# Weight conversion moved out of the last expert slot, softplus of two chunks ahead of a loop

## The chip, the cores and the metric

The kernel runs on 1 core of one Trainium2 chip. The metric is the time of one execution in microseconds (us) of device time. Six engines or queues matter here: TensorE (PE) for matrix products, VectorE (DVE), ScalarE (ACT) and GpSimd (POOL) for elementwise work, and SyncE (SP), which issues most DMAs.

## The reference

Three networks stand one behind the other. An attention over 32 memory slots per head (8 batches, 8 heads, 576 positions) gives 4608 rows of 512 numbers. A router picks one of 8 experts per row, and the expert is a two-layer network, `gate * (relu(x @ w1[e]) @ w2[e])`, with 1024 hidden units. Last comes a network that all rows share:

```
h = x @ w_in            # 4608 x 512 by 512 x 2048
g = max(h, 0) + log1p(exp(-|h|))
out = g @ w_out         # 2048 x 512
```

The weights `w_in` and `w_out` come in as 64-bit floats and have to be made 32-bit floats on the chip. "Conversion" below is this work.

## The kernel before, in words

Products are made exact enough by splitting each operand into a high and a low part and adding three products (`mm3`, L64): lines L67, L68 and L69 are its three matmuls. `split` (L55) makes the parts: ScalarE copies the high part (L58), VectorE or GpSimd subtracts it for the low part (L61).

**Experts** (`experts`, L649 on). Rows are sorted by expert. Eight units of 512 rows (s = 0 to 7) and two slots of 256 rows (s = 8 and 9, `LAST` is 9) are written out as one long list of 80 steps (s, n), n = 0 to 7 being chunks of 128 hidden units. Inside `tc.manual_schedule()` every engine works in the order in which the code is written. A step x holds:

- the first layer of its chunk on TensorE (12 matmuls into a PSUM tile `ph`), then the relu: ScalarE writes the high half of `h` (L125), VectorE the low half (L126);
- weight parts for the next unit: `part(0, m)` splits first-layer weights with VectorE's help, `part(1, m)` second-layer weights with GpSimd's, and loads for the unit after that;
- in steps n = 0 and 1, transposes and splits of the next unit's rows (`turn`, L675); in step n = 2, on SyncE, the loads of the rows of the unit after the next, with register loads ahead of them (`rows_of`);
- one `next(conv)`, in s = 1 to 7 and in s = 9;
- the second layer (`layer2`, tile `py`) of the step two earlier (`LAG = 2`); after a unit's last chunk, `slot_out` scales its rows on ScalarE (L693), GpSimd adds a column (L694) and SyncE stores them (L696).

**Conversion** (`convert`, L714). There are 32 halves of 128 x 512 numbers. Each takes two `yield`s, and the end of a half falls to the call after its second one. A call of the first kind finishes the half before (VectorE L729, which reads GpSimd's sum; then the store to `wsc` L712, or for the first six halves a split into the resident tiles `first`), asks for the load of the half after this one (L706, tile `d`, 2 buffers), and starts its half: VectorE L723 and L724, then ScalarE's Abs (L725), which overwrites what L724 reads. A call of the second kind is VectorE L726 and L727, then GpSimd's add (L728). With 32 halves this makes 64 yields and a 65th call that ends the last half. In the kernel before, units 1 to 7 make 56 calls, slot 9 makes 8, and the rest runs behind the steps.

**The loop** (L820) handles further slots of 256 rows, from a count that routing found on the chip (`nslots`). With these inputs the trace shows no turn of it; all engines meet there all the same, and SyncE also meets the DMAs issued ahead of it. Ahead of it stand the first layers of chunks 0 and 1 of the last network (`begun`, L818).

**The last network** (`last_network`, L872) works through 9 blocks of 512 rows with 16 chunks each: `layer3` (12 matmuls), softplus (three ScalarE operations L908 to L910, four VectorE operations L912 to L915, a split), and two chunks later `layer4` (12 matmuls). During block 0 it loads the weights of chunk 3 and on from `wsc` in halves (L895, tile `s`, 3 buffers under the tag `yt`) and splits them into tiles that the experts have left.

Of the kernel before, what the change touches and what calls it, by code (L numbers as in the profile page):

```python
# [1 line left out]

# [7 lines left out]
F32 = mybir.dt.float32  # L10
F32R = mybir.dt.float32r
BF16 = mybir.dt.bfloat16
I32 = mybir.dt.int32
AF = mybir.ActivationFunctionType
ALU = mybir.AluOpType
# [4 lines left out]
P = 128  # L20
# [4 lines left out]
DM = H * D  # L25
# [3 lines left out]
GC = FF // P  # L29
SLOT = 256  # L30
UNIT = 512
UNITS_E = 8
# [104 lines left out]
@with_exitstack  # L137
def tile_kernel(ctx, tc, qT, kv, phi, mid, wg, mbias, w1, w2, wffn, out):
    nc = tc.nc
    V, A, G, PE, SP = nc.vector, nc.scalar, nc.gpsimd, nc.tensor, nc.sync  # L140

    dram = ctx.enter_context(tc.tile_pool(name="dram", bufs=1, space=DRAM))
    cst = ctx.enter_context(tc.tile_pool(name="cst", bufs=1))

    xs = dram.tile([E * RG, ROW], F32, name="xs")
    ys = dram.tile([PAD + NT, ROW], F32, name="ys")
    wsc = dram.tile([GC, P, 2 * 4 * P], F32, name="wsc")

    A.preload_act_table_set("natural_log_exp_and_others")
    big = ctx.enter_context(tc.tile_pool(name="big", bufs=1))  # L150
    K = lambda i, shape, dt: big.tile([P, *shape], dt, name=f"k{i}", tag="k", bufs=12)
    Q = lambda i, shape, dt: big.tile([P, *shape], dt, name=f"q{i}", tag="q", bufs=3)
    J = lambda i, shape, dt: big.tile([P, *shape], dt, name=f"j{i}", tag="j", bufs=5)
    Z = lambda i, shape, dt: big.tile([P, *shape], dt, name=f"z{i}", tag="z", bufs=1)
    table = cst.tile([1, 4, TAB], I32, name="table")
    few = cst.tile([1, 7], I32, name="few")
    pick = [few[:, 0:3], few[:, 3:6]]
    nslots = few[:, 6:7]

    rows = ExitStack()  # L160
    ps_y = rows.enter_context(tc.tile_pool(name="ps_y", bufs=2, space=PSUM, side="right"))
    ig0 = cst.tile([P, 2, 2], F32, name="ig0")
    weights, py0 = attention_and_routing(tc, locals())
    act = ctx.enter_context(tc.tile_pool(name="act", bufs=1))
    raw = act.tile([P, UNIT // 32, P], F32, name="raw")
    hl = act.tile([P, 2, 2, 4, BLK], F32R, name="hl")
    fst = ctx.enter_context(tc.tile_pool(name="fst", bufs=1, side="right"))
    first = [[fst.tile([P, 1024], F32R, name=f"first{n}_{w}") for w in range(2)] for n in range(3)]
    ids = [act.tile([P, BLK // P], I32, name=f"ids{j}") for j in range(2)]
    idf = act.tile([P, BLK // P], F32, name="idf")  # L170
    ps_3 = ctx.enter_context(tc.tile_pool(name="ps_3", bufs=2, space=PSUM))
    begun = experts(tc, locals())
    rows.close()
    last_network(tc, locals())


# [472 lines left out]
def experts(tc, env):  # L649
# [5 lines left out]
    with ExitStack() as st:  # L655
        pool = lambda name, bufs, **kw: st.enter_context(tc.tile_pool(name=name, bufs=bufs, **kw))
        wk = pool("b_wk", 2)
        cv = pool("b_cv", 1)
        ps_h = pool("b_ps_h", 2, space=PSUM, side="right")

        W = env["weights"]
# [83 lines left out]
        with tc.manual_schedule():  # L745
# [26 lines left out]
            for x in range(len(steps) + LAG):  # L772
                if x < len(steps):
                    s, n = steps[x]
                    if x == 1:
                        slot_out([py0], ig0, PAD + NT - SLOT)
                    k = n - (3 if s == 0 else 0)
                    turned = [turn(s % 2, 2 * k + i, size(s + 1)) for i in range(2)] if s < LAST and k in (0, 1) else []
                    for t in turned:
                        next(t)  # L780
                    hs[x] = layer1((s + 1) % 2, n, size(s))
                    if s == 0:
                        for w, m in ((1, n), (0, n + 2)):
                            if m < FC:
                                part(w, m)
                                if m % 2 == 1 and (w, m) != (0, 1):
                                    load(w, m // 2, *regs[1])
                    for t in turned:
                        next(t)
                    if s + 2 <= LAST and k == 2:  # L790
                        rows_of(s + 2)
                        if s > 0:
                            expert_of(s + 2)
                    for w, ago in ((0, 2), (1, 4)):
                        if x >= ago and steps[x - ago][0] < LAST:
                            after, m = steps[x - ago]
                            part(w, m)
                            if m % 2 == 1 and after + 2 <= LAST:
                                load(w, m // 2, *regs[after + 2])
                    if s == LAST - 1 and n == 3:  # L800
                        block_in(tc, env, 0)
                    if s == LAST and 2 <= n < 6:
                        block_turn(tc, env, wk, 0, n - 2, 2)
                    if s == LAST and n == 6:
                        block_ids(tc, env, 0)
                    if 0 < s < UNITS_E or s == LAST:
                        next(conv, None)
                if x >= LAG:
                    s, n = steps[x - LAG]
                    if n == 0:  # L810
                        py[s] = [ps_y.tile([P, 2, DM], F32, name="py", tag="y") for _ in range(size(s) // SLOT)]
                    layer2(n, py[s], hs.pop(x - LAG))
                    if n == FC - 1:
                        slot_out(py.pop(s), igs.pop(s), PAD + NT - SLOT - UNIT if s == 0 else value(2, entry(s), PAD + NT - size(s)))
            for _ in conv:
                pass
            total = nc.values_load(nslots, min_val=TABU + SLOTS_E, max_val=TAB)
            begun = [layer3(tc, env, ps_3, first[n], 0) for n in range(2)]  # L818

        with tc.For_i(TABU + SLOTS_E, total, 1) as s:  # L820
            e = value(0, s, E - 1)
# [15 lines left out]
                if n + 2 < FC:  # L837
                    h.append(alone(n + 2))
            slot_out([pt], ig, y0)
    return begun  # L840


def layer3(tc, env, pool, w, j):
# [17 lines left out]
    tc.nc.vector.tensor_copy(env["ids"][j % 2], env["idf"])  # L861


def block_turn(tc, env, pool, j, k, bufs):
    nc = tc.nc
    raw, hl = env["raw"], env["hl"]
    yt = pool.tile([P, BLK], F32, name="yt", tag="yt", bufs=bufs)
    nc.vector.transpose(yt.rearrange("p (a b) -> p a b", b=32), raw[:, :, 32 * k:32 * k + 32])
    split(nc, yt, hl[:, (j + 1) % 2, 0, k], hl[:, (j + 1) % 2, 1, k], nc.scalar, nc.vector)


def last_network(tc, env):  # L872
    nc = tc.nc
    V, A, G, PE, SP = nc.vector, nc.scalar, nc.gpsimd, nc.tensor, nc.sync
    wsc, out, first, ids, ps_3, begun = (env[n] for n in ("wsc", "out", "first", "ids", "ps_3", "begun"))

    with ExitStack() as st:
        pool = lambda name, bufs, **kw: st.enter_context(tc.tile_pool(name=name, bufs=bufs, **kw))
        wp = pool("c_w", 1)
        wk = pool("c_wk", 2)  # L880
        ps_h = pool("c_ps_h", 2, space=PSUM)
        ps_o = pool("c_ps_o", 4, space=PSUM)
# [2 lines left out]
        q = [Q(6 + i, (2, 1024), F32R) for i in range(3)]  # L885
        room = [*(K(24 + i, (1024,), F32R) for i in range(12)), *(J(10 + i, (1024,), F32R) for i in range(5)),
                *(x[:, i] for x in q for i in range(2)), Z(2, (1024,), F32R)]
        room += [wp.tile([P, 1024], F32R, name=f"w{i}") for i in range(2 * (GC - len(first)) - len(room))]
        wh, wl = ([first[n][w] if n < len(first) else room[2 * (n - len(first)) + w] for n in range(GC)]
                  for w in range(2))  # L890

        def weights(n):
            for i in range(2):
                s, x = wk.tile([P, 512], F32, name="s", tag="yt", bufs=3), slice(512 * i, 512 * i + 512)
                SP.dma_start(s, wsc[n, :, x])  # L895
                split(nc, s, wh[n][:, x], wl[n][:, x], A, V)

        def hidden(j, n):
            if j == 0 and n < len(begun):
                ph = begun[n]  # L900
            else:
                ph = layer3(tc, env, ps_h if n % 4 // 2 else ps_3, (wh[n], wl[n]), j)
            u = wk.tile([P, BLK], F32, name="u", tag="u")
# [1 line left out]
            c = wk.tile([P, BLK], F32, name="c", tag="c", bufs=1)  # L905
            gh = wk.tile([P, BLK], F32R, name="gh", tag="gh", bufs=3)
            gl = wk.tile([P, BLK], F32R, name="gl", tag="gl", bufs=3)
            A.activation(u, ph, AF.Abs)  # L908
            A.activation(u, u, AF.Exp, scale=-1.0)  # L909
            A.activation(g, u, AF.Ln, bias=1.0)  # L910

            V.tensor_scalar(c, u, 1.0, 1.0, op0=ALU.add, op1=ALU.subtract)  # L912
            V.tensor_tensor(c, c, u, ALU.subtract)  # L913
            V.scalar_tensor_tensor(g, ph, 0.0, g, op0=ALU.max, op1=ALU.add)  # L914
            V.tensor_tensor(g, g, c, ALU.subtract)  # L915
            split(nc, g, gh, gl, A, V)
            return gh, gl

        def layer4(po, g, n):
# [3 lines left out]

        def block_out(j, po):
            for t in range(BLK // P):
                ob = wk.tile([P, DM], F32, name="ob", tag=("yt", "yt", "g", "g")[t], bufs=3)
                A.activation(ob, po[t], AF.Copy)  # L927
                w = G.indirect_dma_start(out, IndirectOffsetOnAxis(ap=ids[j % 2][:, t:t + 1], axis=0), ob, None,  # L928
                                         bounds_check=NT - 1, oob_is_err=False)
# [8 lines left out]
        for x in range(len(steps) + LAG):  # L938
            if x < len(steps):
# [4 lines left out]
                if j + 1 < NBLK:  # L944
# [1 line left out]
                        block_in(tc, env, j + 1)  # L946
                        block_ids(tc, env, j + 1)
                    if n in (6, 8, 10, 12):
                        block_turn(tc, env, wk, j + 1, (n - 6) // 2, 3)
            if x >= LAG:  # L950
                j, n = steps[x - LAG]
                if n == 0:
# [40 lines left out]
```

## Time and profile before

| what | value |
|---|---|
| time, three runs | 1411.44, 1412.92 (median), 1417.55 us |
| profiled execution | 1422.22 us, of which 1420.2 us span |
| mean granted TensorE clock | 0.976 of full |
| PE busy | 1370.2 us (96% of the span) |
| DVE busy | 922.5 us (65%) |
| ACT busy | 674.6 us (48%) |
| POOL busy | 256.9 us (18%) |
| chain that ended last | PE 50%, issue 6%, all else below 1% each |

The stages in the profiled execution, read from the timeline: attention and routing until about 190 us, the units s = 0 to 7 until about 548 us, the slots s = 8 and 9 until 603.76 us, the loop and its neighbours until 618.88 us, the last network to the end. An engine's busy time is an average over these stages; the windows view shows each stage by itself, and the timeline gives for each instruction how long its engine idled before it and what ended that. In rows a step of the units is followed best by its relu on VectorE (L126), of which there is one per step.

### The profile page before, as it was taken

The page shows a single profiled execution, that of the slowest core. Times are in us where ns is not written, and L with a number is a line of the kernel's source. Part 1 is how long each engine was busy: PE and PEld are TensorE (multiplying, and loading weights), DVE is VectorE, ACT ScalarE, POOL GpSimd, SP SyncE. Part 2 cuts the span into 40 slices and gives each one's busy share as a digit, 9 for nine tenths or more (in the row PEclk, how much of TensorE's full clock was granted, in tenths as well). Part 3 has the DMA queues.
Part 4 walks back from the last instruction along what each step waited for, and adds up shares of the span by engine and source line. Part 5 has one row for each costly group of instructions (what it writes and reads, how often), then busy time and mean ns, then how long its engine had stood idle before and what let it go on. Part 6 is the DMA issues. An engine that isn't in the chain of part 4 may idle for free.

```text
span 1420.2 us, 19794 instructions
## 1 busy us (share of the span) xinstructions
PE 1370.2 (96%) x7312; PEld 1100.9 (78%) x7312; DVE 922.5 (65%) x1699; ACT 674.6 (48%) x1193; POOL 256.9 (18%) x267
## 2 busy tenths in 40 slices
PE   7997989999999999889999999999999999999997
PEld 5775758878888888668888888888888888888885
DVE  4665857777877775769665756657566575665553
ACT  3554435444443445356544545445454454544443
POOL 1343314333434334300100101001010010100101
PEclk8889989999999999999999999999999999999998
DMA  9975984445334566244010200202001020000000
GB/s 357 402 285 202 374 240 102 104 113 140 95 99 127 170 213 182 89 143 133 23 38 0 60 1 23 38 0 60 1 23 38 0 60 1 23 8 1 30 1 30
DMA packets 94338, 143.03 MB, mean 101 GB/s; under 512 B 16160, under 2 KB 54048, under 8 KB 94240
## 3 DMA queue, kind: packets, MB, share of 16 engines
q1 hardware_dynamic: 86320, 120.94, 28.5%
q0 software_dynamic: 5760, 19.17, 3.5%
q10 hardware_dynamic: 2160, 1.63, 0.4%
q8 instruction: 58, 0.95, 0.3%
q14 instruction: 40, 0.33, 0.1%
HBM read 122.28 MB, written 44.62 MB: 118 GB/s over the span
## 4 chain that ended last, share of the span: by engine, by line
PE 50%; issue 6%; POOL 0%; DMA 0%; ACT 0%; DVE 0%; POOLq 0%; SPq 0%
PE po L67 8%; PE po L69 8%; PE po L68 8%; PE ph L67 8%; PE ph L69 8%; PE ph L68 8%; POOL out L928 0%; DMA s<-wsc 0%; POOLq L989 0%; ACT u L908 0%; DVE g L914 0%; DVE c L913 0%; ACT u L909 0%; ACT g L910 0%; ACT k L58 0%
## 5 line engine op out<-in xcount | busy, mean ns | idle before, releaser
L67 PE MATMUL ph<-hl,k 128*128 128x512 f32 (+1 forms) x536 | 204.3, 381 | 8.2 <-ACT hl L58 5.4
L68 PE MATMUL ph<-hl,k 128*128 128x512 f32 (+1 forms) x536 | 204.3, 381 | 0.0
L58 ACT ACTIVATE gh<-g 128x512 fp32r<-128x512 f32 x144 | 91.0, 632 | 228.3 <-DVE g L915 228.0
L912 DVE TENSOR_SCALAR c<-u 128x512 f32<-128x512 f32 x144 | 61.5, 427 | 194.7 <-ACT u L909 185.2
L928 POOL DMA_INDIRECT out<-ob,ids x36 | 41.3, 1147 | 767.9 <-ACT ob L927 661.7
L69 PE MATMUL ph<-hl,k 128*128 128x512 f32 (+1 forms) x456 | 173.1, 380 | 0.0
L61 DVE TENSOR_TENSOR gl<-g,gh 128x512 fp32r<-128x512 f32 x144 | 99.2, 689 | 84.7 <-ACT gh L58 83.7
L908 ACT ACTIVATE u<-ph 128x512 f32<-128x512 f32 x144 | 86.1, 598 | 133.0 <-PE ph L69 128.1
L67 PE MATMUL py<-q,h 128*128 128x512 f32 x304 | 121.7, 400 | 6.9 <-ACT h L125 5.9
L67 PEld LDWEIGHTS ph<-hl,k 128*128 128x128 f32 x536 | 101.6, 190 | 31.4 <-ACT hl L58 8.2
L69 PE MATMUL py<-q,h 128*128 128x512 f32 x304 | 120.7, 397 | 0.8 <-DVE h L126 0.8
L68 PEld LDWEIGHTS ph<-hl,k 128*128 128x128 f32 x536 | 101.6, 190 | 21.3 <-DVE hl L61 1.8
L126 DVE SCALAR_TENSOR_TENSOR h<-ph,h 128x512 fp32r<-128x512 f32 (+1 forms) x88 | 54.2, 616 | 82.6 <-ACT h L125 82.4
L913 DVE TENSOR_TENSOR c<-c,u 128x512 f32<-128x512 f32 x144 | 99.6, 692 | 4.5
L915 DVE TENSOR_TENSOR g<-g,c 128x512 f32<-128x512 f32 x144 | 99.0, 688 | 4.2
L914 DVE SCALAR_TENSOR_TENSOR g<-ph,g 128x512 f32<-128x512 f32 x144 | 98.3, 684 | 0.9 <-ACT g L910 0.9
L69 PEld LDWEIGHTS ph<-hl,k 128*128 128x128 f32 x456 | 85.7, 188 | 16.3
L125 ACT ACTIVATE h<-ph 128x512 fp32r<-128x512 f32 (+1 forms) x88 | 47.3, 537 | 107.4 <-PE ph L69 101.1
L909 ACT ACTIVATE u<-u 128x512 f32<-128x512 f32 x144 | 90.8, 631 | 4.0
L910 ACT ACTIVATE g<-u 128x512 f32<-128x512 f32 x144 | 90.8, 631 | 3.9
L67 PE MATMUL po<-k,gh 128*128 128x512 f32 x216 | 85.9, 398 | 0.0
L69 PE MATMUL po<-k,gl 128*128 128x512 f32 x216 | 85.5, 396 | 0.0
(236 smaller groups left out, 3083.7 us busy)
## 6 DMA issues: line engine op xcount, KB each, us to landing
k<-w SPq DMA_DIRECT2D x43, 512.0 KB
j<-w SPq DMA_DIRECT2D x43, 512.0 KB
k<-kv SPq DMA_DIRECT2D x36, 512.0 KB
d<-wffn SPq DMA_DIRECT2D x32, 512.0 KB
q<-qT SPq DMA_DIRECT2D x8, 1152.0 KB
raw<-ys SPq DMA_DIRECT2D x36, 256.0 KB
xs<-zero SPq DMA_DIRECT2D x8, 1056.0 KB
ys<-y SPq DMA_DIRECT2D x8, 1026.0 KB
```

The source lines that it names most:

```text
L58: hi_eng.activation(hi, x, AF.Copy)
L61: lo_eng.tensor_tensor(lo, x, hi.bitcast(F32), ALU.subtract)
L67: nc.tensor.matmul(out, lh, rh, start=start, stop=False)
L68: nc.tensor.matmul(out, lh, rl, start=False, stop=False)
L69: nc.tensor.matmul(out, ll, rh, start=False, stop=stop)
L908: A.activation(u, ph, AF.Abs)
L909: A.activation(u, u, AF.Exp, scale=-1.0)
L910: A.activation(g, u, AF.Ln, bias=1.0)
L912: V.tensor_scalar(c, u, 1.0, 1.0, op0=ALU.add, op1=ALU.subtract)
L913: V.tensor_tensor(c, c, u, ALU.subtract)
L914: V.scalar_tensor_tensor(g, ph, 0.0, g, op0=ALU.max, op1=ALU.add)
L915: V.tensor_tensor(g, g, c, ALU.subtract)
```

## The change

- Each of the units 1 to 7 makes a second `next(conv)` in step n = 3, units 1 and 2 make another one in step n = 6, and slot 9 makes none. That is 56 + 7 + 2 = 65 calls, so conversion ends with unit 7.
- The register loads of the loop's bound (`values_load`) move to step n = 6 of slot 9.
- The softplus of chunks 0 and 1 stands ahead of the loop, in written order, with tiles of the conversion's pool `cv` (tags a, b, c with one buffer each; results in tag d). The first layer of chunk 2 (`ready`) stands there too, as do three loads of weight halves for chunks 3 and 4 (`halves`), into the same tags a, b, c.
- The pool `cv` lives on into the last network. Its tags a, b, c in turn replace the three `yt` buffers, and two of its d buffers hold the last chunk's weights in place of the pool `wp`.

```diff
-    begun = experts(tc, locals())
+    cv = ctx.enter_context(tc.tile_pool(name="cv", bufs=1))
+    begun, ready, halves = experts(tc, locals())
...
                     if s == LAST and n == 6:
                         block_ids(tc, env, 0)
-                    if 0 < s < UNITS_E or s == LAST:
+                        total = nc.values_load(nslots, min_val=TABU + SLOTS_E, max_val=TAB)
+                    if 0 < s < UNITS_E:
                         next(conv, None)
+                        if n == 3 or (s < 3 and n == 6):
+                            next(conv, None)
...
-            for _ in conv:
-                pass
-            total = nc.values_load(nslots, min_val=TABU + SLOTS_E, max_val=TAB)
-            begun = [layer3(tc, env, ps_3, first[n], 0) for n in range(2)]
+            begun = []
+            for n in range(2):
+                ph = layer3(tc, env, ps_3, first[n], 0)
+                g = cv.tile([P, 2, BLK], F32R, name="g01", tag="d", bufs=2)
+                u, c, t = (cv.tile([P, BLK], F32, name=f"{x}01", tag=x) for x in "abc")
+                softplus(nc, ph, u, t, c, g[:, 0], g[:, 1])
+                begun.append((g[:, 0], g[:, 1]))
+            ready = [layer3(tc, env, ps_3, first[2], 0)]
+            halves = [scratch(env, 3 + i // 2, i % 2, i) for i in range(3)]
...
+def scratch(env, n, i, k):
+    s = env["cv"].tile([P, BLK], F32, name="s", tag="abc"[k % 3])
+    env["nc"].sync.dma_start(s, env["wsc"][n, :, 512 * i:512 * i + 512])
+    return s
+
+def softplus(nc, ph, u, g, c, gh, gl):
+    V, A = nc.vector, nc.scalar
+    A.activation(u, ph, AF.Abs)
+    A.activation(u, u, AF.Exp, scale=-1.0)
+    A.activation(g, u, AF.Ln, bias=1.0)
+    V.tensor_scalar(c, u, 1.0, 1.0, op0=ALU.add, op1=ALU.subtract)
+    V.tensor_tensor(c, c, u, ALU.subtract)
+    V.scalar_tensor_tensor(g, ph, 0.0, g, op0=ALU.max, op1=ALU.add)
+    V.tensor_tensor(g, g, c, ALU.subtract)
+    split(nc, g, gh, gl, A, V)
...
         def weights(n):
             for i in range(2):
-                s, x = wk.tile([P, 512], F32, name="s", tag="yt", bufs=3), slice(512 * i, 512 * i + 512)
-                SP.dma_start(s, wsc[n, :, x])
+                s, x = halves.pop(0) if halves else scratch(env, n, i, next(turns)), slice(512 * i, 512 * i + 512)
                 split(nc, s, wh[n][:, x], wl[n][:, x], A, V)
 
         def hidden(j, n):
             if j == 0 and n < len(begun):
-                ph = begun[n]
+                return begun[n]
+            if j == 0 and ready:
+                ph = ready.pop()
```

## Rows read from the trace of the kernel before

**Rows 1.** Windows: us, busy us of each engine (instructions), PE clock, DMA share, GB/s.
```profile
404.00:449.00 45.00, 45.00 (x197) 36.69 (x197) 35.27 (x46) 19.60 (x36) 18.32 (x14) 1.00 0.44 118
582.00:604.00 22.00, 15.29 (x68) 11.53 (x67) 15.16 (x28) 5.73 (x12) 5.22 (x5) 0.84 0.25 89
190.00:200.00 10.00, 9.87 (x25) 6.34 (x26) 4.68 (x7) 4.83 (x9) 1.91 (x2) 0.61 1.12 286
```

**Rows 2.** Timeline, TensorE, end of units and loop: start, us, operation, [idle before <-releaser].
```profile
593.22 0.50 PE L67 MATMUL py<-q,h 128*128 128x512 f32 x1 [2.13 <-ACT h L125]
...
601.04 0.79 PE L67 MATMUL py<-q,h 128*128 128x512 f32 x1 [2.76 <-ACT h L125]
...
603.76 0.48 PE L67 MATMUL ph<-hl,first 128*128 128x512 f32 x1
...
610.51 0.60 PE L68 MATMUL ph<-hl,first 128*128 128x512 f32 x1 [2.07 <-ACT u L908]
...
618.88 0.51 PE L67 MATMUL ph<-hl,k 128*128 128x512 f32 x1 [2.58 <-ACT k L58]
```

**Rows 3.** Timeline, ScalarE: two short steps, a conversion, the loop's exit.
```profile
566.70 0.39 ACT L125 ACTIVATE h<-ph 128x256 fp32r<-128x256 f32 x1 [1.40 <-PE ph L69]
...
569.52 0.39 ACT L125 ACTIVATE h<-ph 128x256 fp32r<-128x256 f32 x1 [1.40 <-PE ph L69]
...
592.24 0.65 ACT L725 ACTIVATE d<-d 128x512 f32<-128x512 f32 x1 [2.54 <-DVE b L724]
...
609.29 0.60 ACT L908 ACTIVATE u<-ph 128x512 f32<-128x512 f32 x1 [3.97 <-SPq L820]
```

**Rows 4.** Timeline, VectorE, units: second half of each relu, one row a step.
```profile
268.89 0.69 DVE L126 SCALAR_TENSOR_TENSOR h<-ph,h 128x512 fp32r<-128x512 f32 x1 [0.93 <-ACT h L125]
...
275.56 0.69 DVE L126 SCALAR_TENSOR_TENSOR h<-ph,h 128x512 fp32r<-128x512 f32 x1 [1.22 <-ACT h L125]
...
398.63 0.69 DVE L126 SCALAR_TENSOR_TENSOR h<-ph,h 128x512 fp32r<-128x512 f32 x1 [1.22 <-ACT h L125]
...
402.61 0.69 DVE L126 SCALAR_TENSOR_TENSOR h<-ph,h 128x512 fp32r<-128x512 f32 x1 [0.54 <-ACT h L125]
...
408.17 0.69 DVE L126 SCALAR_TENSOR_TENSOR h<-ph,h 128x512 fp32r<-128x512 f32 x1 [1.21 <-ACT h L125]
...
413.65 0.69 DVE L126 SCALAR_TENSOR_TENSOR h<-ph,h 128x512 fp32r<-128x512 f32 x1 [0.83 <-ACT h L125]
...
420.26 0.69 DVE L126 SCALAR_TENSOR_TENSOR h<-ph,h 128x512 fp32r<-128x512 f32 x1
...
425.14 0.69 DVE L126 SCALAR_TENSOR_TENSOR h<-ph,h 128x512 fp32r<-128x512 f32 x1 [0.23 <-ACT h L125]
...
430.89 0.69 DVE L126 SCALAR_TENSOR_TENSOR h<-ph,h 128x512 fp32r<-128x512 f32 x1 [1.22 <-ACT h L125]
```

**Rows 5.** Timeline, VectorE and GpSimd: conversion operations and what they waited for.
```profile
404.00 1.78 DVE L729 SCALAR_TENSOR_TENSOR c<-d,a 128x512 f32<-128x512 f32 x1
...
426.83 0.68 DVE L729 SCALAR_TENSOR_TENSOR c<-d,a 128x512 f32<-128x512 f32 x1
...
434.48 1.30 POOL L728 TENSOR_TENSOR a<-a,b 128x512 int32<-128x512 int32 x1 [1.15 <-DVE b L727]
...
439.52 0.43 DVE L723 TENSOR_SCALAR a<-d 128x512 int32<-128x512 int32 x1 [0.56 <-DMA d<-wffn]
```

**Rows 6.** Timeline, SyncE's queue: a chunk's load, the last store ahead of the loop.
```profile
433.69 0.42 SPq L706 DMA_DIRECT2D d<-wffn  x1
...
605.93 0.46 SPq L712 DMA_DIRECT2D wsc<-c  x1
```

**Rows 7.** Timeline, TensorE: the product that reads the relu of 430.89.
```profile
440.83 0.39 PE L69 MATMUL py<-q,h 128*128 128x512 f32 x1
```

**Rows 8.** Timeline, ScalarE and VectorE: one softplus near the kernel's end.
```profile
1401.35 0.60 ACT L908 ACTIVATE u<-ph 128x512 f32<-128x512 f32 x1 [1.18 <-PE ph L69]
...
1405.82 0.69 DVE L61 TENSOR_TENSOR gl<-g,gh 128x512 fp32r<-128x512 f32 x1 [0.70 <-ACT gh L58]
```

More of the change, by code (lines that the diff above doesn't have):

```diff
@@ L1 @@
+import itertools
 from contextlib import ExitStack
@@ L657, in experts @@
         wk = pool("b_wk", 2)
-        cv = pool("b_cv", 1)
+        cv = env["cv"]
         ps_h = pool("b_ps_h", 2, space=PSUM, side="right")
@@ L802, in experts @@
                     if s == LAST and 2 <= n < 6:
-                        block_turn(tc, env, wk, 0, n - 2, 2)
+                        block_turn(tc, env, wk, 0, n - 2, "yt", 2)
                     if s == LAST and n == 6:
                         block_ids(tc, env, 0)
-                    if 0 < s < UNITS_E or s == LAST:
+                        total = nc.values_load(nslots, min_val=TABU + SLOTS_E, max_val=TAB)
+                    if 0 < s < UNITS_E:
                         next(conv, None)
+                        if n == 3 or (s < 3 and n == 6):
+                            next(conv, None)
                 if x >= LAG:
@@ L839, in experts @@
             slot_out([pt], ig, y0)
-    return begun
+    return begun, ready, halves
+def scratch(env, n, i, k):
[12 more added lines that the diff above has]
+    split(nc, g, gh, gl, A, V)
 def layer3(tc, env, pool, w, j):
@@ L861, in block_ids, with block_turn @@
     tc.nc.vector.tensor_copy(env["ids"][j % 2], env["idf"])
-def block_turn(tc, env, pool, j, k, bufs):
+def block_turn(tc, env, pool, j, k, tag, bufs):
     nc = tc.nc
     raw, hl = env["raw"], env["hl"]
-    yt = pool.tile([P, BLK], F32, name="yt", tag="yt", bufs=bufs)
+    yt = pool.tile([P, BLK], F32, name="yt", tag=tag, bufs=bufs)
     nc.vector.transpose(yt.rearrange("p (a b) -> p a b", b=32), raw[:, :, 32 * k:32 * k + 32])
@@ L874, in last_network @@
     V, A, G, PE, SP = nc.vector, nc.scalar, nc.gpsimd, nc.tensor, nc.sync
-    wsc, out, first, ids, ps_3, begun = (env[n] for n in ("wsc", "out", "first", "ids", "ps_3", "begun"))
+    out, first, ids, ps_3, cv = (env[n] for n in ("out", "first", "ids", "ps_3", "cv"))
+    begun, ready, halves = (env[n] for n in ("begun", "ready", "halves"))
     with ExitStack() as st:
         pool = lambda name, bufs, **kw: st.enter_context(tc.tile_pool(name=name, bufs=bufs, **kw))
-        wp = pool("c_w", 1)
         wk = pool("c_wk", 2)
@@ L887, in last_network @@
                 *(x[:, i] for x in q for i in range(2)), Z(2, (1024,), F32R)]
-        room += [wp.tile([P, 1024], F32R, name=f"w{i}") for i in range(2 * (GC - len(first)) - len(room))]
+        room += [cv.tile([P, 1024], F32R, name=f"w{i}", tag="d", bufs=2) for i in range(2)]
         wh, wl = ([first[n][w] if n < len(first) else room[2 * (n - len(first)) + w] for n in range(GC)]
                   for w in range(2))
+        turns = itertools.count(len(halves))
         def weights(n):
             for i in range(2):
-                s, x = wk.tile([P, 512], F32, name="s", tag="yt", bufs=3), slice(512 * i, 512 * i + 512)
-                SP.dma_start(s, wsc[n, :, x])
+                s, x = halves.pop(0) if halves else scratch(env, n, i, next(turns)), slice(512 * i, 512 * i + 512)
                 split(nc, s, wh[n][:, x], wl[n][:, x], A, V)
@@ L907, in hidden @@
             gl = wk.tile([P, BLK], F32R, name="gl", tag="gl", bufs=3)
[L908 to L916, printed above, removed]
+            softplus(nc, ph, u, g, c, gh, gl)
             return gh, gl
@@ L925, in block_out @@
             for t in range(BLK // P):
-                ob = wk.tile([P, DM], F32, name="ob", tag=("yt", "yt", "g", "g")[t], bufs=3)
+                if t < 2:
+                    ob = cv.tile([P, DM], F32, name="ob", tag="abc"[next(turns) % 3])
+                else:
+                    ob = wk.tile([P, DM], F32, name="ob", tag="g", bufs=3)
                 A.activation(ob, po[t], AF.Copy)
@@ L948, in last_network @@
                     if n in (6, 8, 10, 12):
-                        block_turn(tc, env, wk, j + 1, (n - 6) // 2, 3)
+                        block_turn(tc, env, cv, j + 1, (n - 6) // 2, "abc"[next(turns) % 3], 1)
             if x >= LAG:
```

## The prediction

> **What bounds the kernel now.** I read the windows first, then the timelines of TensorE, ScalarE and VectorE where a window shows TensorE idle. Over one unit TensorE is busy all 45.00 us at full clock (197 matmuls, 0.23 us each), VectorE 35.27 and ScalarE 19.60 [rows 1]. So in the units TensorE sets the end and VectorE has a fifth of its time free. In 582 to 604 us, slot 9, TensorE is busy 15.29 of 22.00 us and its clock falls to 0.84 [rows 1]. The idle times there end with the relu on ScalarE: 2.13 and 2.76 us [rows 2]. ScalarE itself stood at the conversion's Abs, which waited 2.54 us for VectorE's L724 [rows 3]. So conversion bounds slot 9. Then comes the loop. The first matmul ahead of it is at 603.76, the flow stops until 610.51, stops again until 618.88 [rows 2], and ScalarE leaves the loop at 609.29 after 3.97 us for SyncE [rows 3]. From there on TensorE bounds. The change can win only between 570 and 619 us; it puts the work into the units.
>
> **Slot 9: what is removed.** Eight conversion calls leave it. A short step takes 2.82 us when nothing disturbs it (relus at 566.70 and 569.52, both waiting for TensorE), and the second relu is that of slot 9's step 0 [rows 3]. Seven more steps bring step 7's relu to 569.52 + 19.74 = 589.26; the second layers of steps 5, 6 and 7 are left, 18 matmuls at 0.23, so the first matmul ahead of the loop can come at 593.4. It came at 603.76 [rows 2]: **10.4 us** to win. It is all won if nothing else is late: block 0's transposes stay, about 2.4 us of VectorE in a step of 2.82 (relu, transpose, ScalarE's copy, remainder at 0.4 to 0.7 each). Lower bound: TensorE's idle time alone, 22.00 - 15.29 = 6.7 us [rows 1].
>
> **The units: what is added.** Seven units get one call more, the first two get two. The calls run on VectorE in written order, so the next step's relu stands behind them, and ScalarE's next relu stands behind the Abs, which waits for VectorE. What a step costs VectorE once it is behind is read from relu to relu [rows 4]:
> - a call of the second kind: 398.63 to 402.61 less 0.54 of waiting for TensorE's products: 3.44 us;
> - of the first kind: 402.61 to 408.17, 5.56 (with 1.21 at the end in which VectorE waits for Abs and relu); with a split into `first` 268.89 to 275.56, 6.67, so 1.1 more;
> - a unit's step 0 with a call of the first kind: 413.65 to 420.26, 6.61; step 1: 4.88; step 2: 5.75; step 7 with the next unit's transposes and a second-kind call: 408.17 to 413.65 less 0.83, 4.65.
>
> TensorE's step is half of 402.61 to 413.65, both waits for TensorE: 5.52 us [rows 4].
>
> In units 1, 2, 3, 5 and 7 the two calls of step 3 are a second kind and then a first kind (ten calls each in units 1 and 2, nine in 3 and on, counted from the first). They follow on each other directly, so VectorE waits for GpSimd's add: relu 430.89, add at 434.48, 1.30 long [rows 4, 5], so L729 can start 4.92 after the relu; with 0.71 L723 could start at 5.63, and from L723 to the next relu it is 441.9 - 439.52 = 2.38 (0.43, L724's 0.7, 1.21 of waiting). That makes 8.0 us. But L723 needs the load that step 2 asked for, behind the row loads on SyncE's queue: issued 433.69, and VectorE got on at 439.52 after waiting for it [rows 5, 6]. That is 8.63 after the relu of 430.89, not 5.63. SyncE's order is tied to VectorE's by GpSimd's add of step 1, behind which the rows' column and store stand, so the load moves with the delay. So step 3 takes 8.63 + 2.38 = **11.0 us**, 5.5 more than TensorE's. In step 6 of units 1 and 2 the load has had a step more: 8.0, in unit 1 with the split 9.1.
>
> How late may a relu be? That of 430.89 ended at 431.58, and the matmul that reads it ran at 440.83 [rows 4, 7]: 9.25, and it was 0.7 late itself: **9.9 us**. Adding up (step less 5.52): unit 1 from 0: step 3 +5.5, step 4 -2.1, 5 +1.2, 6 +3.6, 7 -0.9: 7.2 late. Unit 2: step 0 +2.2 (with a split), 1 -0.6, 2 +0.8, 3 +5.5, 4 -2.1, 5 0, 6 +2.5, 7 -0.9: 14.6. Unit 3: +1.1, -0.6, +0.2, +5.5: **20.8**, the peak, since from step 4 on units come out even or gain. TensorE loses 20.8 - 9.9 = **10.9 us**, in stops behind step 3 of units 2 and 3. Each stop brings a spell at half clock: 0.84 over 22 us is 7.0 us at half, two spells [rows 1], so up to 1.7 us each; only the last counts, and I take 1.2. Bounds: without the load wait the same walk (8.0 in step 3) peaks at 11.9, 2.0 us lost; with all slack held, 0; a gain is excluded, as TensorE is full there. I take 10.9, since the load's row is there in the trace.
>
> The row of L729 in that double step is a choice too: the same operation took 1.78 at 404.00 and 0.68 at 426.83 [rows 5]. I took 0.7, as in the double step it starts when GpSimd has just ended the add it waits for. The Trainium skill ("SBUF — State Buffer", section "SBUF: two separate sides") says that a VectorE operation with two SBUF operands and a GpSimd operation hold a shared port pair one at a time, the later one blocked for the whole instruction. By that rule 0.7 holds in a double step; priced at 1.78, step 6 of units 1 and 2 would add 2.2 and the sum would be 2.2 higher.
>
> **The loop: what is moved.** Count from T, the first matmul ahead of the loop. Now 36 first-layer matmuls are done and TensorE flows again at T + 15.1 (603.76 to 618.88) [rows 2]. Afterwards the same 36 stand ahead of the loop and take 8.3 us; the loop must not end before the two softplus and the three loads. Chunk 0's products are ready at T + 3.05 (12 at 0.23, 0.3 for the end). One softplus runs from 1401.35 to 1405.82 + 0.69: 5.16, and its copy to `gh` starts 0.70 ahead of the last part, at 3.8 [rows 8]. The second softplus on ScalarE starts behind that copy, at T + 3.05 + 4.3, and ends at T + 12.5. Its last tile, c, is the third load's target, so that load is issued at T + 12.6. At the loop all engines wait for SyncE, and SyncE for its DMAs: the last store went out at 605.93 and ScalarE was out at 609.29, 3.36 later, TensorE at 610.51, 4.58 later [rows 2, 3, 6]. TensorE comes early to the loop now, so I take 3.36: flow at T + 16.0, **0.9 later** than now. Bounds: -2.1 if the load's landing cost nothing, +2.1 with 4.58. What goes is the chain behind the loop (softplus, splits): the second layer of chunk 0 can start at once, and its 2.8 us cover the split of chunk 3. But TensorE has stood for 7 to 8 us. In 190 to 200, after the wait at the start of the units, the clock was 0.61 [rows 1], 7.8 us at half, which costs 3.9; a short stop costs 1.7. I take **2.8**. The first softplus also holds the PSUM buffer of chunk 2's products, for about 0.6 us, inside the wait.
>
> At nothing: three tags with one buffer each in place of three buffers of one tag, for the same rotation; two d buffers in place of the pool `wp`; the register loads a step earlier. TensorE's flow from 622 us on hides them; if a rotation stalled, a load of about 3 us per weight half would show in block 0. The two softplus taken out of block 0 free VectorE and ScalarE there, where TensorE bounds: nothing.
>
> **Sum.** -10.4 (slot 9) + 10.9 + 1.2 (units) + 0.9 + 2.8 (loop) = +5.4 us against the profiled execution, 1422.22 us (span 1420.2 and 2.0 around it), so 1427.6. The median of the runs is 1412.92, 9.3 below that execution; the difference carries over: **1418.3 us**, 0.4% slower, inside what a measurement can tell from no change (0.5%, 7 us).
>
> **Rivals.**
> 1. The units hide the calls. For it: VectorE has 9.7 us free per unit [rows 1], and without the load wait the walk loses 2.0. Against: the row of the wait [rows 5]. -10.4 + 2.0 + 0.9 + 2.8 = -4.7: 1408.2; with nothing lost and the loop at its lower price (-2.1, 1.7), down to 1402.1.
> 2. Slower: GpSimd. Its add in a double step stands behind its weight split (1.3 us), and L729 is held as at 404.00 (1.1 more). In step 3 the load's wait covers this, in step 6 of units 1 and 2 it doesn't: 2 x 2.4 = +4.9, and 1423.2. It decides as soon as a double step without load wait takes over 10 us, relu to relu. For it: 1.78 is a frequent length. Against: GpSimd's split starts ahead of the calls, so it should be done.
> 3. The loop gives nothing of the change's purpose back in another way: the loads hold it (4.58) and the clock stays low (3.9): +2.3 on the forecast, 1420.6; part of the slow side.
>
> **How the numbers follow.** The forecast (units lose 6 to 14 us) has 0.5, and by itself 1412 to 1422. Rival 1 has 0.3, rivals 2 and 3 together 0.2. Faster by over 0.5% means below 1405.9: half of rival 1, 0.15. Slower means above 1420.0: rivals 2 and 3 and the forecast's upper quarter, 0.33. The rest, 0.52, is no change. The range reaches from inside rival 1 to beyond rival 2: 1404 to 1426.
>
> **What would show it.** Slot 9 at full flow, 2.8 us a step; doubled steps of about 11 us between relus in step 3 of units 1, 2, 3, with a wait for the load of d at L723; TensorE idle for some 5 us in units 2 and 3, then low clock; TensorE's flow about 16 us behind T, starting with a second layer and at half clock. It is wrong if TensorE's windows in units 2 and 3 stay full, if L723 does not wait, or if the loop ends before T + 14.

## The result, and the profile after

The changed kernel takes 1430.76 us (median of 4 runs, 1429.91 to 1431.71), the kernel before 1412.18 (4 runs, 1411.37 to 1417.55): ratio 1.0128, 95% interval 1.0110 to 1.0147. It is 18.6 us slower; 5.4 were predicted. The profiled execution took 1429.91 us, span 1428.2. Its line numbers are one or two higher: the relus are L126 and L127, the row scalings L695, the conversion L725 to L731, the split L59 and L62.

Windows of the changed kernel (us, busy us of each engine, granted clock, DMA share, GB/s), the first two in the place of [rows 1]:

```profile
404.00:449.00 45.00, 45.00 (x197) 36.71 (x196) 37.03 (x46) 20.13 (x37) 18.35 (x14) 1.00 0.39 108
582.00:604.00 22.00, 22.00 (x142) 19.89 (x141) 10.10 (x18) 12.10 (x25) 10.29 (x10) 1.00 0.38 84
359.00:404.00 45.00, 40.48 (x168) 32.55 (x167) 36.22 (x45) 18.64 (x35) 17.85 (x13) 0.92 0.41 110
268.00:314.00 46.00, 37.62 (x156) 30.27 (x155) 34.13 (x46) 19.88 (x36) 16.78 (x13) 0.89 0.38 97
```

The slots are full now, at full clock. Some units are full as before. The other two windows lost 4.5 and 8.4 us of TensorE's time, with the clock at 0.92 and 0.89: 0.11 of 46 us is 10 us at the lower of the two levels. The waits between 222 and 560 us (engine, operation, what it waited for: us in total, times, longest) show what TensorE's stops have in common, first in the changed kernel, then in the kernel before:

```profile
ACT d L727 <- DVE b L726: 107.2, 26, 8.8
...
PE py L68 <- ACT y L695: 23.9, 4, 8.4
```

```profile
PE py L67 <- ACT y L693: 1.0, 1, 1.0
```

One such stop of 1.0 us was there before. TensorE's timeline of the changed kernel has the four stops, and the loop:

```profile
289.09 0.80 PE L68 MATMUL py<-q,h 128*128 128x512 f32 x1 [8.38 <-ACT y L695]
...
340.14 0.80 PE L68 MATMUL py<-q,h 128*128 128x512 f32 x1 [4.82 <-ACT y L695]
...
390.98 0.80 PE L68 MATMUL py<-q,h 128*128 128x512 f32 x1 [4.52 <-ACT y L695]
...
487.79 0.80 PE L68 MATMUL py<-q,h 128*128 128x512 f32 x1 [6.15 <-ACT y L695]
...
614.66 0.39 PE L68 MATMUL ph<-hl,first 128*128 128x512 f32 x1
...
621.86 0.50 PE L68 MATMUL ph<-hl,first 128*128 128x512 f32 x1 [2.14 <-issue]
...
625.92 0.40 PE L68 MATMUL po<-first,g 128*128 128x512 f32 x1
...
1417.00 0.39 PE L70 MATMUL po<-w,gl 128*128 128x512 f32 x1
```

Each stop stands at a unit's first second-layer product and ends with a row scaling of the unit before. A unit of 512 rows takes both `py` accumulators (`ps_y` has two buffers), so the next unit's second layer can't begin until ScalarE has scaled and emptied them. ScalarE's timeline at the first stop, changed kernel:

```profile
282.16 0.63 ACT L59 ACTIVATE first<-c 128x512 fp32r<-128x512 f32 x1 [2.37 <-DVE c L731]
284.66 0.66 ACT L727 ACTIVATE d<-d 128x512 f32<-128x512 f32 x1 [1.87 <-DVE b L726]
285.22 0.58 ACT L126 ACTIVATE h<-ph 128x512 fp32r<-128x512 f32 x1
285.70 1.14 ACT L59 ACTIVATE hl<-xt 128x512 fp32r<-128x512 f32 x2
286.74 0.62 ACT L59 ACTIVATE k<-k 128x512 fp32r<-128x512 f32 x1
287.26 0.61 ACT L59 ACTIVATE q<-j 128x512 fp32r<-128x512 f32 x1
287.78 2.41 ACT L695 ACTIVATE y<-py,ig 128x512 f32<-128x512 f32 x4
```

The scalings run at 287.78; what they read had long been finished. Ahead of them in ScalarE's order stand a split and an Abs of the conversion and copies of transposed rows, all of which wait for VectorE, which is late.

The times by stage. The two executions differ by about 9.5 us before the units, so the units are counted from the first layer of the fourth step of unit 0 (TensorE's timeline, before and after) to the first matmul of slot 8, and the end is the last matmul:

```profile
204.55 0.39 PE L67 MATMUL ph<-hl,k 128*128 128x512 f32 x1
...
542.51 0.28 PE L67 MATMUL ph<-hl,k 128*128 128x256 f32 x1
...
1409.28 0.39 PE L69 MATMUL po<-w,gl 128*128 128x512 f32 x1
```

```profile
195.02 0.39 PE L68 MATMUL ph<-hl,k 128*128 128x512 f32 x1
...
563.92 0.28 PE L68 MATMUL ph<-hl,k 128*128 128x256 f32 x1
```

| stretch | before | after | difference | predicted |
|---|---|---|---|---|
| units, to slot 8 | 337.96 | 368.90 | +30.9 | +12.1 |
| slots, to T (first matmul ahead of the loop) | 61.25 | 50.74 | -10.5 | -10.4 |
| T to the last matmul | 805.52 | 802.34 | -3.2 | +3.7 |
| sum | | | +17.2 | +5.4 |

### The profile page after: what moved, and what is told of

Read it like the earlier page. It is cut to its first block, busy times and chain, and to the rows that moved or that the text cites. A ratio compares the mean times of both kernels' runs of the same rounds, so it can differ in the third digit from the quotient of the medians.

```text
span 1428.2 us, 19767 instructions
## 1 busy us (share of the span) xinstructions
PE 1362.0 (95%) x7312; PEld 1095.3 (77%) x7312; DVE 929.5 (65%) x1699; ACT 674.8 (47%) x1193; POOL 257.5 (18%) x267
## 4 chain that ended last, share of the span: by engine, by line
PE 50%; issue 6%; POOL 0%; ACT 0%; POOLq 0%; DVE 0%
PE ph L68 8%; PE po L68 8%; PE ph L70 8%; PE ph L69 8%; PE po L70 8%; PE po L69 8%; POOL out L956 0%; POOLq L1017 0%; ACT u L862 0%; ACT u L863 0%; ACT g L59 0%; DVE c L869 0%; DVE c L866 0%; POOLq L956 0%
## 5 line engine op out<-in xcount | busy, mean ns | idle before, releaser
L59 ACT ACTIVATE gh<-g 128x512 fp32r<-128x512 f32 x142 | 89.6, 631 | 236.8 <-DVE g L869 236.2
L62 DVE TENSOR_TENSOR gl<-g,gh 128x512 fp32r<-128x512 f32 x142 | 98.2, 691 | 88.0 <-ACT gh L59 88.0
L68 PE MATMUL py<-q,h 128*128 128x512 f32 x304 | 124.0, 408 | 23.9 <-ACT y L695 23.9
L70 PE MATMUL py<-q,h 128*128 128x512 f32 x304 | 122.2, 402 | 0.0
L127 DVE SCALAR_TENSOR_TENSOR h<-ph,h 128x512 fp32r<-128x512 f32 (+1 forms) x88 | 54.1, 614 | 82.4 <-ACT h L126 81.9
L68 PEld LDWEIGHTS py<-q,h 128*128 128x128 f32 x304 | 59.0, 194 | 38.8 <-ACT y L695 25.6
```

The source lines that it names most:

```text
L59: hi_eng.activation(hi, x, AF.Copy)
L62: lo_eng.tensor_tensor(lo, x, hi.bitcast(F32), ALU.subtract)
L68: nc.tensor.matmul(out, lh, rh, start=start, stop=False)
L70: nc.tensor.matmul(out, ll, rh, start=False, stop=stop)
```

## The experiments

"TensorE's stops" are its idle times over 0.3 us in a trace; each kernel ran beside the kernel before on the same chip.

**The two halves of the change.** Theory: the units lose all that is lost.

```
# one: the changed kernel with the calls of before
-                    if 0 < s < UNITS_E:
+                    if 0 < s < UNITS_E or s == LAST:
                         next(conv, None)
-                        if n == 3 or (s < 3 and n == 6):
-                            next(conv, None)
...
+            for _ in conv:
+                pass
# two: the kernel before with the changed calls, nothing else
```

> The changed kernel with the conversion calls where they were (one per step in units 1 to 7 and in slot 9, the rest behind the steps): the loop's part of the change alone. From the two profiles the stretch from the first matmul ahead of the loop to TensorE's steady flow fell from 15.1 to 11.3 us and the last network's rest grew by about 1. Theory (the units lose, the loop's part wins a little): 3 to 4 us below before, about 1409. Rival (the softplus and loads ahead of the loop are what costs): over 1420.

> The kernel before with the changed calls alone (two in step 3 of units 1 to 7 and in step 6 of units 1 and 2, none in slot 9). Theory: the units lose about 31 us as in the changed kernel (four stops of TensorE, 23.9 us, and four spells at half clock), slot 9 wins 10.5: about 1432. Rival: under 1420.

The first took 0.9978 of before [0.9964, 0.9992], the second 1.0108 [1.0078, 1.0139], with the stops of the changed kernel again (waits, 222 to 560 us, of the second):

```profile
PE py L67 <- ACT y L693: 24.1, 4, 8.5
```

From unit 1's first matmul to slot 8's TensorE took 531.61 - 221.26 = 310.35 us in the first and 561.45 - 220.10 = 341.35 in the second: 31.0 us more without any alignment. Of these, 23.1 are stops (24.1 against 1.0 in the first); the rest, 7.9, is for the most part half clock behind them. The loss is the units' alone.

**Abs taken from ScalarE.** The mask gives the same numbers on VectorE.

```
-                       A.activation(m, m, AF.Abs))
+                       V.tensor_scalar(hi, hi, 0x7FFFFFFF, None, op0=ALU.bitwise_and))
```

> The changed kernel with the conversion's Abs as a mask on VectorE (0.43 us more for each of 32 halves there) in place of an activation on ScalarE, so that no ScalarE instruction of the later halves waits for VectorE. Theory (TensorE stands at the accumulators that ScalarE has to empty, and ScalarE is late only because Abs holds it behind VectorE): most of the 31 us in the units goes, 1400 to 1408. Rival (VectorE is simply overloaded and its relus come too late): VectorE has more to do, so 1428 or more.

> The kernel before with the Abs as a mask on VectorE. Theory: the units stay full, slot 9 loses less than its 10 us because ScalarE's relus no longer stand behind VectorE: 1405 to 1410. Rival (VectorE's load sets slot 9): 1412 to 1417.

In the changed kernel: 0.9954 [0.9933, 0.9974], 1407.19 us, as the theory expected; in the kernel before 0.9985 [0.9971, 0.9999], 1411.99 us, less than expected and at the rival's edge: slot 9 goes on stopping (1.53, 1.11 and 2.13 us), now for VectorE. With the mask VectorE has more to do than in the changed kernel, and yet 17.6 of the 23.9 us are gone from the units. So what costs there is not that VectorE is late, but that ScalarE waits for it. What is left (waits, same stretch):

```profile
PE py L68 <- ACT y L695: 6.3, 2, 5.5
```

**More calls earlier in a unit.** If lateness is paid at the unit's start, it should help to be done with the calls by then.

```
-                        if n == 3 or (s < 3 and n == 6):
+                        for _ in range((0, 1, 2, 2, 2, 2, int(s < 3), 0)[n]):
```

> The changed kernel with the same nine or ten calls per unit, put into steps 1 to 5 (one, then two each; units 1 and 2 one more in step 6) and none in steps 7 and 0, with the same operations. Theory (what counts is how late ScalarE and VectorE are at step 1 of the next unit, when the row scalings must empty the accumulators; a relu in mid-unit may be 9.9 us late): VectorE catches up by 9 us in the steps without calls, the stops at the unit starts go, 1400 to 1408. Rival (the amount of VectorE work per unit costs, or the lateest relu does): the peak in mid-unit is higher than before, so 1428 or more.

1.0114 [1.0093, 1.0134], 1430.85 us: nothing won, the theory's number missed, and the rival's (1428 or more) came. The traces say why. The waits and ScalarE's timeline at the largest stop:

```profile
PE py L68 <- ACT y L695: 19.1, 5, 7.1
PE py L68 <- ACT h L126: 3.7, 3, 1.7
```

```profile
293.26 0.63 ACT L59 ACTIVATE first<-c 128x512 fp32r<-128x512 f32 x1 [2.37 <-DVE c L731]
295.72 0.65 ACT L727 ACTIVATE d<-d 128x512 f32<-128x512 f32 x1 [1.82 <-DVE b L726]
296.27 2.40 ACT L695 ACTIVATE y<-py,ig 128x512 f32<-128x512 f32 x4
```

The edit left a call in step 1, ahead of the scalings, where its split and its Abs hold them by themselves. And four doubled steps in a row made the relus late enough to stop TensorE in mid-unit, for 1.60, 1.68 and 0.46 us, as the rival had it; that is 3.7 us beside the 19.1 at the scalings.

**The calls in later units, Abs on VectorE.**

```
-                        if n == 3 or (s < 3 and n == 6):
+                        if s > 2 and (n == 3 or (s < 7 and n == 6)):
```

> Abs on VectorE, and the nine extra calls only in units 3 to 7 (step 3 of each, step 6 of units 3 to 6), so units 1 and 2, whose halves ScalarE splits into resident tiles, keep one call per step. Theory: the 5.5 us stop that is left with Abs on VectorE comes from those splits (ScalarE waited up to 6.2 us for VectorE's L731 there) and goes; slot 9 stays full; 1398 to 1402. Rival (VectorE's load): two calls in two steps of one unit bring the stops back in units 4 to 7, 1410 or more.

0.9965 [0.9953, 0.9978], missed: 1410.09 us, the rival's number, and no better than with the changed calls. The stops moved to the later units' starts and come now from the copies of the transposed rows, which stand ahead of the scalings too (ScalarE waited 4.18 and 4.19 us for VectorE's transposes ahead of the stops of 3.19 and 3.42):

```profile
PE py L68 <- ACT y L695: 10.0, 4, 3.4
```

**The order on ScalarE.** These decide it: the same 65 calls, Abs on ScalarE as in the changed kernel, but the scalings ahead of all that waits for VectorE (first kernel), or ahead of the calls alone (second). A third is the first with Abs on VectorE.

```
-                    k = n - (3 if s == 0 else 0)      # transposes in steps 0, 1
+                    k = n - (3 if s == 0 else 2)      # first kernel only: steps 2, 3; rows' loads in step 4
...
-                        next(conv, None)
-                        if n == 3 or (s < 3 and n == 6):
+                        for _ in range((0, 0, 1, 1, 2, 1, 1 + (s < 3), 1)[n]):
                             next(conv, None)
...
                         slot_out(...)
+                        if s < UNITS_E - 1:
+                            for _ in range(2):
+                                next(conv, None)
```

> The changed kernel with another order in the units: the next rows' transposes stand in steps 2 and 3 (loads of rows in step 4), and no call of the conversion stands ahead of the row scalings: two calls behind slot_out in step 1, one in steps 2, 3, 5, 6 and 7, two in step 4, one more in step 6 of units 1 and 2. So 65 calls as in the changed kernel, nine or ten a unit, but everything that stands ahead of the scalings in ScalarE's order waits for TensorE alone. Theory (late VectorE work reaches TensorE only through ScalarE's order, Abs or copies ahead of the row scalings that must empty the two accumulators): the stops of 8.4, 4.8, 4.5 and 6.2 us at the starts of units go, units take 44.2 us each, slot 9's 10.5 us stay won and the end comes at T + 802.4: some 13 below before, 1397 to 1403. Rival A (VectorE simply has too much work, its late relus stop TensorE by themselves): stops ended by L126, 1415 or more. Rival B (the accumulators are taken too late whatever stands ahead): stops ended by L695 stay, 1420 or more.

> As the kernel sent beside it, but the transposes stay in steps 0 and 1 as they were: only the calls are moved behind the row scalings (two behind slot_out in step 1, then 1, 1, 2, 1, 1 and 1 in steps 2 to 7, one more in step 6 of units 1 and 2). Theory: the ScalarE copies of the transposed rows (L59) still stand ahead of the scalings and wait for VectorE's transposes, which are as late as VectorE is; no Abs does. So smaller stops at the starts of units, ended by L695, some 1 to 3 us each: 1402 to 1414. If Abs alone was what held the scalings: no stops, 1397 to 1403. If neither order matters: 1425 or more.

> As the first kernel of this call, with the conversion's Abs as a mask of the sign bit on VectorE. Theory: with the scalings free of VectorE nothing is left for this to win, and VectorE has 0.7 us more per half: the same within 2 us of the first kernel, 1397 to 1404. Rival (Abs on ScalarE also costs by holding ScalarE's relus): 3 or more below the first kernel.

The first: 1406.77 us, where the kernel before took 1423.05 on this chip: 0.9889 [0.9870, 0.9909], 16.3 us below it where 13 were expected. The second 0.9956 [0.9942, 0.9970], with stops where its theory put them; the third 0.9914 [0.9892, 0.9935], not to be told from the first. TensorE's waits between 222 and 560 us, first and second kernel:

```profile
PE py L68 <- ACT h L126: 1.1, 1, 1.1
```

```profile
PE py L68 <- ACT y L695: 4.3, 2, 3.9
```

With VectorE just as loaded (window of the first kernel: 41.16 us busy in 45, against 37.03 above) TensorE is full:

```profile
404.00:449.00 45.00, 45.00 (x197) 36.72 (x196) 41.16 (x51) 21.19 (x40) 21.61 (x15) 1.00 0.48 138
```

In the second kernel ScalarE shows what holds the scalings when no Abs does:

```profile
287.67 1.23 ACT L59 ACTIVATE hl<-xt 128x512 fp32r<-128x512 f32 x2 [2.61 <-DVE xt L677]
...
291.26 1.22 ACT L59 ACTIVATE hl<-xt 128x512 fp32r<-128x512 f32 x2 [0.84 <-DVE xt L677]
...
293.43 2.40 ACT L695 ACTIVATE y<-py,ig 128x512 f32<-128x512 f32 x4
```

So the mechanism is shown, in both its parts (Abs, and the copies of transposed rows), and by its ratio to before the first kernel beats both the kernel before and the changed one.

**The loop.** First the loop's part by itself (old calls), without its loads (`halves = []`), and with its loads alone (no softplus and no third first layer ahead):

> The loop's part alone, as in e1, without the three weight loads ahead of the loop. Theory (the loads are written ahead of the loop but run behind it, since their tiles are those of the second softplus): the same as e1 within 1.5 us, 1410 to 1412.5. Rival (the loads win the time): 2 to 4 us slower than e1.

> The loop's part alone with the loads, but both softplus and chunk 2's first layer behind the loop as in the kernel before. The tiles a, b, c are then free when conversion ends, so the loads can run ahead of the loop. Theory (the softplus wins the 3 us): 1412 to 1415, as before. Rival (the loads win it): 1409 to 1411.

Both took 0.9977 of before ([0.9962, 0.9992] and [0.9962, 0.9993]), as the whole loop part did (0.9978). The first came out as its theory had it, the second did not: the loads are not needed for the gain, nor are the softplus. The three don't differ, so no piece is shown to win. From T to the last matmul they took 804.6, 804.9 and 805.1 us, 0.4 to 0.9 less than before; the timed 3 us (1 to 5 by the intervals) are not all found there, and where the rest comes from stays open. Common to the three kernels are the earlier register loads and the shared pool; neither was tried alone. Then the other way round, the new order of the units in the kernel before:

> The kernel before with the units' order of the run that took the transposes and the calls behind the row scalings (65 calls, conversion over with unit 7), and nothing of the rest of the change: no softplus, third first layer or loads ahead of the loop, no shared pool. In the traces the end came 805.5 us after T in the kernel before, 802.3 in the changed one, 805.1 with the loop's part alone and 802.4 with the changed calls alone. Theory (the 3 us behind T come from conversion being over when slot 9 begins, and the code ahead of the loop wins nothing of its own): T + 802 to 804, ratio within 0.2% of that run's 0.9889. Rival (the code ahead of the loop wins 3 us by itself): T + 805.5 and a ratio of 0.991 to 0.992.

1400.83 us against 1413.44: 0.9909 [0.9885, 0.9932]. By time it can't be told from 0.9889. By the trace the theory holds (TensorE's timeline, T, the loop, the last matmul):

```profile
585.16 0.39 PE L67 MATMUL ph<-hl,first 128*128 128x512 f32 x1
...
591.90 0.50 PE L68 MATMUL ph<-hl,first 128*128 128x512 f32 x1 [2.14 <-DVE c L916]
...
1386.90 0.39 PE L69 MATMUL po<-w,gl 128*128 128x512 f32 x1
```

That is T + 801.7 with the old loop, where the changed kernel has 802.3. One trace each would prove little, as this stretch varies by some 2 us. But in all nine traces in which conversion is over before slot 9 it took 801.7 to 804.1 us, and in the five others 804.6 to 807.8; the two of the nine above 803 (804.1 and 803.6) lost some of it to a spell at the lower clock behind the loop. The two traces with the old loop (801.7 and 802.4) are not behind those with the new one. So the 3.2 us behind T come from conversion being over before slot 9, and no gain of the code put ahead of the loop shows in them.

## Why the prediction was wrong

**Slot 9: right.** 10.4 predicted, 10.5 measured, with TensorE full (582 to 604 us above against 15.29 of 22.00 in [rows 1]) and 2.82 us from relu to relu.

**The doubled steps: right to about 1 us.** 11.0 us between relus were predicted for step 3, with a wait for the load. VectorE's timeline of the changed kernel, units 1 and 2:

```profile
243.23 0.69 DVE L127 SCALAR_TENSOR_TENSOR h<-ph,h 128x512 fp32r<-128x512 f32 x1 [1.21 <-ACT h L126]
...
244.44 1.78 DVE L728 SCALAR_TENSOR_TENSOR a<-d,b 128x512 int32<-128x512 int32 x1
...
248.15 0.69 DVE L731 SCALAR_TENSOR_TENSOR c<-d,a 128x512 f32<-128x512 f32 x1 [1.47 <-POOL a L730]
...
250.83 0.43 DVE L725 TENSOR_SCALAR a<-d 128x512 int32<-128x512 int32 x1 [0.60 <-DMA d<-wffn]
...
253.24 0.69 DVE L127 SCALAR_TENSOR_TENSOR h<-ph,h 128x512 fp32r<-128x512 f32 x1 [1.25 <-ACT h L126]
...
297.42 0.69 DVE L127 SCALAR_TENSOR_TENSOR h<-ph,h 128x512 fp32r<-128x512 f32 x1 [1.62 <-ACT h L126]
...
305.64 0.43 DVE L725 TENSOR_SCALAR a<-d 128x512 int32<-128x512 int32 x1 [2.61 <-DMA d<-wffn]
...
308.05 0.69 DVE L127 SCALAR_TENSOR_TENSOR h<-ph,h 128x512 fp32r<-128x512 f32 x1 [1.25 <-ACT h L126]
```

10.0 and 10.6 us, each wait where it was expected. Only the slow operation is another: L728 took 1.78, while L731, for which the choice between 1.78 and 0.7 was weighed, took 0.69 (in the kernel before the same question stood at [rows 5]). The Trainium skill ("SBUF — State Buffer", section "SBUF: two separate sides") agrees: L728 began while GpSimd was at a weight split (244.32, 1.36 long), L731 when its add had just ended.

**"How late may a relu be? 9.9 us": the step that failed.** That slack is the one in mid-unit [rows 4, 7], and no run shows it far wrong: in mid-unit a relu stopped TensorE only where four doubled steps stood in a row, and for 1.1 us in the kernel with the new order. But it was used for the whole unit. At a unit's start another wait ends first: both accumulators must be emptied by ScalarE, behind Abs and copies that wait for VectorE. Only 12 first-layer products, 2.8 us, lie there between the last product that the scalings read and the first that needs an emptied accumulator, and TensorE went on 1.3 us after the first scaling began (287.78 and 289.09 above). So ScalarE may be late there by some 1.5 us, an estimate from these two, and not by 9.9. The kernel before already stopped there once, for 1.0 us (its row of waits above).

In the prediction's terms, lateness was added up over three units to 20.8 and 9.9 taken off once. What happens is that nearly all of a unit's lateness is paid at the start of the next one, and then it begins anew. Counted at 5.52 us a step from the last relu that VectorE did in time, its relu behind the scalings was 9.3, 5.7, 5.1 and 7.0 us late at the four stops, which took 8.38, 4.82, 4.52 and 6.15 us. Up to the first stop the sum of lateness itself was right: 7.2 us predicted for unit 1 and 1.6 for steps 0 and 1 of unit 2. At the starts of units 4 and 6 the sum lacked something: step 1 took 8.8 us from relu to relu there, 3.3 more than TensorE's. With nine calls a unit from unit 3 on, a call of the first kind stands in that step, and its Abs comes right ahead of the scalings (ScalarE's timeline, changed kernel); the prediction had a step 1 with the other kind alone, at 4.88.

```profile
389.12 0.67 ACT L727 ACTIVATE d<-d 128x512 f32<-128x512 f32 x1 [3.56 <-DVE b L726]
389.69 2.39 ACT L695 ACTIVATE y<-py,ig 128x512 f32<-128x512 f32 x4
```

Stops came to 23.9 us instead of 10.9. The four spells of half clock behind them cost 7.4 us (35 products took 15.6 us where they take 8.2 at full clock), where one spell at 1.2 was predicted.

**The loop: wrong as well, the other way.** "The loop must not end before the two softplus and the three loads" did not hold. TensorE came out of the loop at T + 7.2, and the prediction had named an end before T + 14 as the sign of its being wrong. Though all of this code is written ahead of the loop, in the compiled order the branch stands behind 21 of the 36 first-layer matmuls, with only a part of chunk 0's softplus ahead of it: TensorE's semaphore waits of the loop (L830) lie between 619.8 and 621.6 us, inside the stop. The second softplus and all three loads come behind the branch. The first of the loads, on SyncE's queue:

```profile
626.33 2.48 SPq L856 DMA_DIRECT2D s<-wsc  x2
```

That the change doesn't do what it says there was not among the rivals, though [rows 2] hinted at it: the product behind the stop at 610.51 is still one of the first layer, the 20th of 24. Nor was the clock lost for 2.8 us: TensorE came out of a stop of 2.14 and not of 7 to 8. And the terms left out the other side: in the kernel before, TensorE stops a second time, 2.58 us at 618.88, and is slowed on both sides of the loop (products of 0.48 and 0.60 us in [rows 2], against 0.39 above), while conversion runs up to it. In the last kernel, with the same old loop and no call in slot 9, there is neither a second stop over 0.3 us nor such a slow stretch.

**The rivals.** None of the three was it. The second, GpSimd's hold in step 6 of units 1 and 2, had its own sign, a doubled step without load wait of over 10 us; these steps took 9.3 and 8.1. GpSimd does hold VectorE elsewhere: L731 took 1.76 us at 386.14, ahead of the Abs at 389.12 above, so about 1.1 us of lateness at that stop may be its; no run takes it away by itself. The third, the loop, lost nothing: T to the end became shorter. The first one, that the units hide the calls, becomes true with the other order on ScalarE: 0.9889 of before is beyond its 1408.

## What to carry to other kernels

That an engine has a fifth of its time free does not yet mean that it can take more work. Look along the queues of the engines that wait for it in order, for a waiting instruction behind which stands something that empties an accumulator; with nothing urgent behind such a wait, VectorE at 41 of 45 us stopped TensorE once in the units, for 1.1 us. Read the slack at every kind of place in the loop, above all where one tile ends and all buffers turn over, and not at one step in the middle; the smallest one decides, and it is paid once per turn. And see where a piece of code written ahead of a loop stands in the compiled order before pricing what it holds up.

## What the runs showed of the hardware

Each of the four stops of 4.5 to 8.4 us left TensorE at the lower level of its clock (1.2 GHz, granted 0.50) for 6.7 to 10.2 us; the stop's own end is among them, and 3.2 to 4.4 us of products behind it. So the stops cost some 30% more than they lasted (7.4 us on 23.9). The stop at the loop, 2.14 us long in each of three kernels, had no such spell behind it in the changed kernel and in the last one, and 3.4 us of slow products in the kernel with the new order, whose last network was 1.8 us longer than the changed kernel's. What decides between the two is not shown.
